# Gated delta rule plus MLP on one core: the first chunk in two halves of tokens, PSUM banks of their own, a new order

## The chip, the cores and the metric

One core of one Trainium2 chip runs the whole program. The metric is device time in microseconds (us) for one execution; lower is better. Before the change three runs took 520.83 to 522.82 us, the median 521.94.

## The reference

Two blocks follow each other. The first is a delta rule over 4 x 8 heads, 768 tokens, head size 48:

```python
k_n = k / (np.linalg.norm(k, axis=-1, keepdims=True) + 1e-06)
for t in range(S):
    kt, vt, bt = (k_n[:, :, t], v[:, :, t], beta[:, :, t, None])
    y[:, :, t] = np.einsum('bhd,bhde->bhe', q[:, :, t], state)
    v_old = np.einsum('bhde,bhd->bhe', state, kt)
    state = state + bt[:, :, :, None] * np.einsum('bhd,bhe->bhde', kt, vt - v_old)
```

Its output, with heads put side by side (384 numbers a token), is `x` of the second block:

```python
xn = (x - mu) / np.sqrt(var + 1e-06) * g_ln
ch = np.maximum(xn @ w_ch1, 0.0) @ w_ch2      # 384 -> 1536 -> 384
return x + ch
```

The weights come as 64-bit floats; everything is computed in 32 bits.

## The kernel before

The 768 tokens are cut into 12 chunks of 64. A chunk holds 64 tokens of 32 heads, two of the four batches in the upper 64 partitions and two in the lower, so a tile of MLP rows has 256 tokens (two groups g of 128 rows). Within a chunk the recurrence is written with matrices: the Gram matrix of the keys (`gram`, products L819), the inverse of a triangular matrix made from it, the product of that inverse with the values, called u, and y from u, the masked products of queries and keys (`queries`, L819 and L850) and the state.

The inverse is made in three ways. For chunk 0 `first_inverse` does it by doubling: steps n = 1 to 5, each with products E (L770), a masked copy (L775), products Z (L786), transposes on VectorE (`nat`, L735) and copies on ScalarE (`back`, L729). Step n joins blocks of 2^n tokens. For chunk 1 VectorE eliminates blocks of 16 row by row (`rows_inverse`, L907 and L914), and two joins on TensorE follow (`blocks_join` L938 to L956, `join` L970 to L999). Later chunks are eliminated in blocks of 32, two chunks at a time, with one join. The eliminated blocks go to DRAM (xd) and come back (xt<-xd) in eight transfers for chunk 1; the data to be eliminated come by gb<-gd.

`recur(c)` then does u (L1069 for chunk 0; L1052 and L1057 for chunk 1; L1088 later), y (L1095), the state (L1105), the copy of y to x, layer norm (L1139 to L1151), transposes (L1183 for early chunks) and the scaled transposed rows `xnt`. `mlp(c)` follows. For chunk 0 it has 24 tiles of 128 rows by 128 hidden units (L1406), ReLU on ScalarE (L1414), and 24 products with the second weights (L1448). Chunks 1 and 2 use 256 rows (L1426) and a product scheme with seven instead of eight block products (`seven`, L1523). From chunk 3 on the first layer uses a scheme with fifteen block products (`fifteen`, L1307).

The weights arrive in twelve pieces of 64-bit words. `fetch` loads a piece in two transfers issued by ScalarE; `convert` makes 32-bit floats of it with two ScalarE instructions (L592 hi, L600 lo), one on VectorE (L597) and one on GpSimd (L610). Pieces 0 to 5 are the first weights. Pieces 0 and 1 lie in the buffer of the hidden units, the others in three buffers of their own. Pieces 0 to 2 are converted in halves; an L1406 tile f needs the first halves for f = 0 to 2, the second halves for f = 3 to 5, pieces 3 to 5 from f = 6 on.

What sets the order: every step is recorded by `line.add` with the engine it runs on, and `ORDER`, a list of step numbers, says in which order the steps are emitted. Each engine takes its instructions in that order; waits follow from the data. Numbers count the steps as the code creates them. An "f" in the list puts in a matmul whose result nobody reads.

PSUM has eight banks: the pair `two`, the pair `by`, and f0 to f3. `PAIRS` holds them as pairs. Queries of chunk 2 and later use `two`, as do the products of keys with the state, u, the state and the Gram products; `by` holds the products of queries with the state and y.

## Time and profile before

| | |
|---|---|
| median of three runs | 521.94 us (520.83 to 522.82) |
| the profiled execution | 520.78 us, of which its span is 519.1 us |
| granted TensorE clock, mean | 0.982 |
| TensorE busy in 0 to 20, 20 to 40, 40 to 50, 50 to 60 us | 11.56, 13.59, 7.57, 7.60 us |
| DMA engines' busy share in the same stretches | 1.02, 0.74, 0.83, 0.70 |
| TensorE's last product starts its last long run | 501.88 us (82 records of L1523, 13.34 us) |
| moved | 54.56 MB, 105 GB/s over the span |

Times within the execution count from the start of the span. The profiled execution is one run; its span leaves out 1.68 us around it. A record is one instruction of the trace; most 32-bit matmuls with 128 columns of weights leave two. "issue" marks a wait for which the profile shows no cause. A busy TensorE may also be waiting between two pipelined matmuls, since their ends are modelled.

### The profile page before, as it was taken

The page shows a single profiled execution, that of the slowest core. Times are in us where ns is not written, and L with a number is a line of the kernel's source. Part 1 is how long each engine was busy: PE and PEld are TensorE (multiplying, and loading weights), DVE is VectorE, ACT ScalarE, POOL GpSimd, SP SyncE. Part 2 cuts the span into 40 slices and gives each one's busy share as a digit, 9 for nine tenths or more (in the row PEclk, how much of TensorE's full clock was granted, in tenths as well). Part 3 has the DMA queues.
Part 4 walks back from the last instruction along what each step waited for, and adds up shares of the span by engine and source line. Part 5 has one row for each costly group of instructions (what it writes and reads, how often), then busy time and mean ns, then how long its engine had stood idle before and what let it go on. Part 6 is the DMA issues. An engine that isn't in the chain of part 4 may idle for free.

```text
span 519.1 us, 22785 instructions
## 1 busy us (share of the span) xinstructions
PE 487.1 (94%) x9972; PEld 448.9 (86%) x9972; DVE 360.8 (70%) x814; ACT 206.9 (40%) x462; POOL 280.3 (54%) x447
## 2 busy tenths in 40 slices
PE   5577888999899999999999999999999999999997
PEld 4466786768798889999999989999999999999996
DVE  6577739798887567988889986757988446244241
ACT  5587845423431333234242632533513514424130
POOL 3435654604554877976764274473453742564554
PEclk9878998999999999999999999999999999999999
DMA  9957876585515866345853356643404403003011
GB/s 135 294 115 204 191 154 178 107 195 95 90 26 141 156 134 109 68 88 141 167 120 55 83 108 157 132 81 66 102 10 111 104 17 93 4 1 100 2 39 30
DMA packets 181635, 54.56 MB, mean 105 GB/s; under 512 B 164888, under 2 KB 177312, under 8 KB 181536
## 3 DMA queue, kind: packets, MB, share of 16 engines
q1 hardware_dynamic: 168512, 40.10, 37.9%
q10 hardware_dynamic: 10816, 9.83, 6.6%
q0 software_dynamic: 2208, 3.17, 3.8%
q8 instruction: 78, 1.28, 1.0%
q14 instruction: 21, 0.17, 0.1%
HBM read 36.30 MB, written 16.78 MB: 102 GB/s over the span
## 4 chain that ended last, share of the span: by engine, by line
PE 79%; DMA 5%; SPq 3%; issue 3%; DVE 3%; ACT 3%; POOL 2%; ACTq 0%; DVEq 0%; POOLq 0%
PE f L1523 27%; PE f L1307 22%; PE f L1426 6%; PE f L1448 3%; SPq L410 3%; PE two L819 3%; PE by L1033 2%; PE two L1033 2%; PE by L1095 2%; DMA xnt<-xld 2%; PE two L1088 2%; PE f L1406 1%; PE two L1105 1%; DMA words<-in_moe_w_ch_dram 1%; DMA gb<-gd 1%
## 5 line engine op out<-in xcount | busy, mean ns | idle before, releaser
L1510 POOL TENSOR_TENSOR h_all<-h_all 128x256 f32<-128x256 f32 x99 | 72.7, 745 | 30.5 <-PE f L1523 13.8
L1523 PE MATMUL f<-w_sb,h_all 128*128 128x192 f32 x396 | 82.2, 331 | 1.0 <-ACT h_all L1334 0.6
L1523 PE MATMUL f<-words,h_all 128*128 128x192 f32 x396 | 76.7, 329 | 0.0
L1523 PEld LDWEIGHTS f<-w_sb,h_all 128*128 128x128 f32 x396 | 65.1, 190 | 3.0 <-ACT h_all L1334 1.6
L1330 DVE TENSOR_TENSOR h_all<-f,h_all 128x512 f32<-128x512 f32 x72 | 48.9, 685 | 26.4 <-PE f L1307 19.3
L1523 PEld LDWEIGHTS f<-words,h_all 128*128 128x128 f32 x396 | 65.0, 190 | 1.5 <-issue 0.5
L1548 POOL TENSOR_TENSOR words<-h_all 128x128 f32<-128x128 f32 x66 | 31.2, 491 | 63.4 <-ACT h_all L1334 30.4
L907 DVE TENSOR_TENSOR tmp<-xb,gb 128x31 f32<-128x31 f32 (+19 forms) x139 | 57.5, 413 | 3.9 <-POOL xb L894 0.3
L1325 ACT COPY h_all<-f 128x512 f32<-128x512 f32 x45 | 26.2, 586 | 82.4 <-PE f L1307 68.8
L914 DVE TENSOR_TENSOR xb<-xb,tmp 128x31 f32<-128x31 f32 (+19 forms) x139 | 52.6, 378 | 3.7
L410 POOL DMA_DIRECT2D tb<-in_k_dram x64 | 42.2, 662 | 0.3 <-POOL tb L1630 0.3
L1334 ACT ACTIVATE h_all<-h_all 128x512 f32<-128x512 f32 x54 | 32.7, 626 | 23.9 <-DVE h_all L1330 23.5
L1307 PE MATMUL f<-x_new,w_sb 128*128 128x128 f32 x288 | 40.3, 278 | 0.1
L1307 PE MATMUL f<-xnt,w_sb 128*128 128x128 f32 x288 | 40.2, 277 | 0.0
L1307 PEld LDWEIGHTS f<-x_new,w_sb 128*128 128x128 f32 x288 | 36.5, 191 | 0.6 <-issue 0.2
L1307 PEld LDWEIGHTS f<-xnt,w_sb 128*128 128x128 f32 x288 | 36.5, 192 | 0.6 <-issue 0.2
L1541 DVE TENSOR_TENSOR o<-f,x 128x192 f32<-128x192 f32 x33 | 11.4, 352 | 36.8 <-PE f L1523 30.9
L1426 PE MATMUL f<-xnt,w_sb 128*128 128x256 f32 x144 | 34.5, 387 | 1.4 <-issue 1.4
L1426 PEld LDWEIGHTS f<-xnt,w_sb 128*128 128x128 f32 x144 | 26.4, 190 | 5.4 <-issue 1.8
L1523 PE MATMUL f<-w_sb,words 128*128 128x192 f32 x132 | 26.3, 329 | 0.0
L682 POOL TENSOR_TENSOR v<-v,kpair 128x768 f32<-128x768 f32 x10 | 14.7, 1473 | 14.0 <-DVE pt L897 14.0
L610 POOL TENSOR_TENSOR w_sb<-words 128x768 uint32<-128x768 uint32 (+1 forms) x11 | 14.7, 1348 | 13.7 <-ACT words L600 10.2
(239 smaller groups left out, 983.4 us busy)
## 6 DMA issues: line engine op xcount, KB each, us to landing
words<-in_moe_w_ch_dram ACTq DMA_DIRECT2D x20, 384.0 KB, 4.5
gd<-gsb SPq DMA_DIRECT2D x11, 512.0 KB, 3.9
v<-in_v_dram SPq DMA_DIRECT2D x24, 192.0 KB, 4.2
kr<-in_k_dram SPq DMA_DIRECT2D x46, 96.0 KB, 3.4
out_dram<-o SPq DMA_DIRECT2D x46, 96.0 KB, 2.2
xld<-xlt SPq DMA_DIRECT2D x9, 384.0 KB, 2.4
xnt<-xld SPq DMA_DIRECT2D x36, 96.0 KB, 2.9
tb<-in_q_dram SPq DMA_DIRECT2D x40, 64.0 KB, 2.8
```

The lines of the kernel that those rows point to most:

```text
L410: add(eng, cost, lambda: QUEUE[eng].dma_start(out=out_, in_=in_), r, w, bulk=n * ns / 16e3, np=n, **kw)
L907: lambda j=j, n=n, w=w, t=t: nc.vector.tensor_tensor(out=t, in0=xv[:, 0:n, j : j + 1].to_broadcast([128, n, w]), in1=gv[:, j : j + 1, j + ...
L914: "DVE", dve(n * w), lambda t=t, rest=rest: nc.vector.tensor_tensor(out=rest, in0=rest, in1=t, op=ALU.subtract),
L1033: nc.tensor.matmul(dst[half(e), hp, j], src[drows(hp), (e if n else key_half(c, hp, e)) * GP + j], s_all[drows(hp), e, j], start=(n == 0 o ...
L1307: nc.tensor.matmul(wide(p[:, f : f + 128]), w[:, f : f + 128], r, start=start and i == 0, stop=True, skip_group_check=True)
L1325: add("ACT", act(512), lambda: nc.scalar.copy(o, p), pk, ok)
L1330: add("DVE", dve(512), lambda: nc.vector.tensor_tensor(out=o, in0=x, in1=y, op=op), [*xk_, *yk], ok)
L1334: add("ACT", act(512), lambda: nc.scalar.activation(o, o, ACTF.Relu, scale=scale), [], ok)
L1426: nc.tensor.matmul(p[:, 0:TOK], w1_sb[:, t, f * 128 : (f + 1) * 128], xnt[:, t], start=(t == 0), stop=(t == KC - 1))
L1510: add(eng, cost, lambda: e.tensor_tensor(out=out_, in0=x, in1=y, op=op), r, w, port=2 if eng == "Pool" else 1, pr=-2)
L1523: lambda f=f, t=start and f == order[0]: nc.tensor.matmul(p[:, 0:D2], lhs(f), rhs[:, f], start=t, stop=(f == order[-1]), skip_group_check=True
L1548: lambda f=f + i: e.tensor_tensor(out=s3[f], in0=one(0, 0)[0](f), in1=one(1, 0)[0](f), op=ALU.subtract),
```

## The change

The doubling for chunk 0 stops after step 4, so it yields the inverse of two blocks of 32 tokens. The other block is handled in `first_tokens`: u of the diagonal blocks gives y, layer norm, transposes and `xnt` of the first 32 tokens of every head; the lower block's correction (products w0 and x0) is added to the same PSUM sums, and the second 32 tokens follow. The 24 tiles of chunk 0's MLP go by halves of tokens (u) instead of groups (g), with rows in two runs of 64 columns, and chunk 0's output leaves in eight transfers instead of four. The query transposes of chunk 0 move from step 2 to step 3 of the doubling, the query products from step 5 to step 4, each half of heads in a pair of banks of its own. From chunk 2 on the query products go to `by` instead of `two`, and from chunk 6 on the join's second products to the second bank of `by`. The Gram preparation of chunks 2 and 3 is created after `recur(0)`, and all of `ORDER` is new. Masks move to another buffer, and mask 5 and one set of copies (pts[1]) go.

Cut to its core:

```diff
-        for n in range(1, 6):
+        for n in range(1, 5):
...
-                if n < 5:
+                if n < 4:
                     nat(g, src, Z[2:4])
...
+    def first_queries(**kw):
+        products(0, 1, PAIRS[:2], halves=True, **kw)
+        for g in range(2):
...
+                    out=jn(pts[0])[:, :, js], in0=v[:, :, js], in1=pmask[:, None, None, :].to_broadcast([128, 2, NP, C]), op=ALU.mult,
...
     def join(c, **kw):
-        bank, ATT = (f_[2], FK[2]) if c < LATER else (by[:, 0], BY[:2])
+        banks = [(f_[2], FK[2])] * 2 if c < LATER else [(by[:, 0], BY[:2]), (by[:, 1], BY[2:])]
...
+    def first_tokens(xt, vv, vk, pt, us, x, y_j, **kw):
...
+                        nc.tensor.matmul(
+                            pu[half(e ^ hp), hp, j], xt[half(e), h], vv[half(e), h], start=(j == 0), stop=False, skip_group_check=True
+                        )
+            pe(32, prod_u, vk + [("xt", 0, g, n) for n in range(3)], pk, 0.32, name="u0", **kw)
+            add("ACT", act(384), lambda g=g, pu=pu: nc.scalar.copy(ut[:, g]..., pu), pk, [UT[g]], **kw)
+            scaled(g, pu, pk)
...
+            pe(32, prod_w, [("g", 0, g), UT[g]], [k_ for k_ in WK if k_[2] == g], 0.08, name="w0", **kw)
...
+                    "ACT" if e else "DVE", ... FK[2 + hp], [("wt", hp, e)], after=WT[hp], name="wt", **kw,
...
+        def norm_and_turn(u, banks, pk, turns):
+            rows = half(u)
...   # copies y out (ACT and DVE), statistics, sqrt, reciprocal, normalize, two transposes, xnt on DVE
+        pe(64, lambda: y_of(0, [bank_of(0), bank_of(1)]), ..., YK, 0.32, name="y0", **kw)
+        norm_and_turn(0, [bank_of(0), bank_of(1)], FK[0:2], [(f_[2], FK[2]), (f_[3], FK[3])])
+        for g, (pu, pk) in enumerate(pus):
...
+            pe(32, prod_x, ..., pk, 0.08, name="x0", **kw)
+            scaled(g, pu, pk)
+        pe(64, lambda: y_of(1, y1), ..., BY, 0.4, name="y0", **kw)
+        norm_and_turn(1, y1, [BY[:2], BY[2:]], [(two[:, 0], TWO[:2]), (two[:, 1], TWO[2:])])
...
-        for g, f in ((g, f) for g in range(0 if c else 2) for f in range(FT)):
+        for u, f in ((u, f) for u in range(0 if c else 2) for f in range(FT)):
...
-                        p[:, 0:128], w1_sb[:, t, f * 128 : (f + 1) * 128], xnt[:, t, cols], start=(t == 0), stop=(t == KC - 1)
+                        p[:, 0:128].rearrange("p (g x) -> p g x", g=2), w1_sb[:, t, f * 128 : (f + 1) * 128], tokens(xnt[:, t], u),
...
-            2: lambda: first_kt(tb[1], tb_nat(1), qts[0], ("qt", 0), PAIRS[1], pr=-99),
-            5: lambda: queries(0, PAIRS[1], halves=True, pr=-100),
+            3: lambda: first_kt(tb[1], tb_nat(1), qts[0], ("qt", 0), None, pr=-99),
+            4: lambda: first_queries(pr=-100),
...
-    prep_g(1)
     line.tag = "c0"
     recur(0, -100)
+    prep_g(1)
...
-        queries(c, pr=pr - 1, lag=0.5)
+        queries(c, PAIRS[1], pr=pr - 1, lag=0.5)
```

The new `ORDER` puts TensorE's steps of the front in this sequence: E1 (first half), chunk 1's Gram products, E1 (second half), Z1, E2, Z2, E3, the query transposes, Z3, E4, query products and Z4 by turns, u0, w0, y of the first half, x0, y of the second half, the first half's transposes, key transposes of chunk 2, the first MLP tile, chunk 2's Gram products, the second tile, the second half's transposes, key transposes of chunk 3, the third tile, chunk 3's Gram products, the state, the fourth tile. On VectorE the elimination for chunk 1 stands after the last `xnt` of the first half (before, it stood after the scaling of u), and the convert of the second half of weight piece 1 behind that elimination.

## The prediction

> **What bounds the kernel now.** I read the page first, then the table by windows, then TensorE's timeline, then VectorE's and GpSimd's up to 62 us. TensorE is busy for 94% of the span.
>
> ```profile
> PE 487.1 (94%) x9972; PEld 448.9 (86%) x9972; DVE 360.8 (70%) x814; ACT 206.9 (40%) x462; POOL 280.3 (54%) x447
> ```
>
> ```profile
> 20.00:40.00 20.00, 13.59 (x486) 11.77 (x486) 12.37 (x28) 13.61 (x31) 5.48 (x9) 0.74 0.74 185
> ...
> 50.00:60.00 10.00, 7.60 (x256) 6.61 (x250) 8.75 (x34) 8.27 (x18) 3.46 (x5) 1.00 0.70 210
> ...
> 360.00:380.00 20.00, 20.00 (x497) 19.30 (x496) 18.86 (x37) 8.67 (x18) 9.23 (x17) 1.00 0.44 93
> ```
>
> The columns are stretch, length, then busy time of PE, weight loads, DVE, ACT, POOL, granted clock, DMA share, GB/s. The loss is at the front. The late part holds none: each of the nine last chunks has 120 records of L1307 (100 take 11.3 us in the chain), 84 of L1523 (82 take 13.34 us) and eight small blocks of 0.7 to 1.1 us: 13.6 + 13.7 + 8 = 35 us; (515.2 - 202.7) / 9 = 34.7 us is what a chunk takes. So the end moves with the time at which dense work begins, which I take as chunk 1's first MLP product (L1426).
>
> ```profile
> 24.26 1.54 PE L628 MATMUL by<-ident,tb 128*128 128x128 f32 x6 [2.54 <-issue]
> 25.73 1.99 PE L786 MATMUL f<-xt,gsb 64*64 64x64 f32 x64
> ...
> 36.30 0.81 PE L786 MATMUL f<-xt 64*64 64x64 f32 x32 [0.36 <-DVE xt L775]
> 36.96 0.69 PE L770 MATMUL by<-qt,gsb 64*64 64x64 f32 x32
> ...
> 39.10 1.11 PE L819 MATMUL by<-qt,kt 48*64 48x64 f32 x64
> ...
> 46.04 0.85 PE L1069 MATMUL by<-v,xt 64*64 64x48 f32 x32
> ...
> 59.23 2.27 PE L1406 MATMUL f<-xnt,w_sb 128*128 128x128 f32 x18
> ...
> 62.93 6.21 PE L1406 MATMUL f<-xnt,w_sb 128*128 128x128 f32 x54
> ...
> 86.26 5.19 PE L1448 MATMUL f<-w_sb,h_all 128*128 128x384 f32 x10
> ...
> 114.57 10.63 PE L1426 MATMUL f<-xnt,w_sb 128*128 128x256 f32 x48
> ```
>
> Columns: start, length, what; in brackets the wait ahead of it. One sees the inverse by doubling (L770, L786), its fifth step from 36.96, chunk 0's first product u (L1069) at 46.04, its first MLP tile (L1406) at 59.23, the fourth tile at 62.93, and chunk 1's MLP at 114.57. From 62.93 to 114.57 there are 51.6 us. The work in them: 126 records of L1406 at 0.115, 14.5; 48 of L1448 at 0.325, 15.6; L944 and L949 2.7; L981 and L987 1.4; two blocks of L1033 1.9; u of chunk 1 2.2; L1095 and L1105 1.8; three of L819 3.1; L1183 0.8; sum 44.0. So 7.6 us are lost there; ten L1448 records that take 5.19 instead of 3.25 hold 1.9 of it, a wait in L987 that the profile puts down to issue 1.7.
>
> VectorE's timeline:
>
> ```profile
> 48.19 0.11 DVE L907 TENSOR_TENSOR tmp<-xb,gb 128x15 f32<-128x15 f32 x1
> ...
> 55.88 0.19 DVE L914 TENSOR_TENSOR xb<-xb,tmp 128x15 f32<-128x15 f32 x1
> ```
>
> and GpSimd's:
>
> ```profile
> 61.01 0.82 POOL L610 TENSOR_TENSOR w_sb<-h_all 128x384 uint32<-128x384 uint32 x1 [0.28 <-ACT h_all L600]
> ```
>
> VectorE's elimination for chunk 1 runs from 48.19 to 56.07. The last convert that tiles 4 to 6 need ends at 61.83.
>
> **The change, part by part.** I read the new order engine by engine, numbering the steps as the code creates them.
>
> *The fifth doubling goes.* Z4 ends at 37.11, u starts at 46.04. Ahead of u there now stand only the query products, 1.1 us on PE (L819), and three copies on ACT of 0.36. So u could start at 37.11 + 1.1 + 1.1 = 39.3.
>
> *The front.* The query transposes leave the place between E2 and Z2. Z2's operand was ready at 22.1 (L775, 21.40 + 0.73) and Z2 began at 25.73: 3.6 us, a stall of 2.54 and 1.1 of transposes. They return ahead of Z3, 1.1 to 1.5. E1's first half no longer stands behind chunk 1's products. Against that, ACT's new order puts a convert of weights ahead of the copies of Z1, and that needs two weight transfers; such a transfer took 3.5 to 7.3 us here, with the DMA engines full to 26.5 us. Bounds: 1 us lost to 6 won. I take 3.0, nearest to the 3.6 less the transposes plus E1's advance. u then starts at 36.3.
>
> *The halves of tokens.* From u to the normalized first half the new chain is VectorE's, in its order: u 1.5 on PE; two scalings 0.56 with a convert 0.94 between, 2.1 less the 0.6 under u; convert 0.42; two copies for the second block 1.0; output copy 0.5; small ones 0.4 and convert 0.7; two statistics with aggregates 1.5; scaling 0.56, reciprocal 0.17, normalize 0.48, scaling 0.56; small 0.35, convert 0.94, normalize 0.48; gb 0.41; output copy 0.5; xnt 0.37; two statistics 1.1; memset 0.27; xnt 0.37: 14.1, with some twenty hand-overs (0.07 each, an estimate) 15.5. The three new products and the second pair of transposes (about 3 us of PE, against 2.0 for the doubling's E5 and Z5) lie under that chain. Its cover is PE's idleness here; without it they would cost 1 us net. First tile: 36.3 + 15.5 = 51.8, against 59.23.
>
> *What stands behind it.* The elimination now follows xnt in VectorE's order: from 51.6. It took 7.9 with 1.8 of other work inside; the second half's normalization, 1.4, now lies inside. End 59.6. Behind it in the same queue is the convert of weight piece 1's second half (0.4 to 1.0), then GpSimd's 0.82: the fourth tile at 61.0, 1.9 sooner. But chunk 1's query transposes, its query products and its state product (1.1 + 1.16 + 1.15 = 3.4 us) were done by 62.93 and now are not. So PE is 1.5 us behind there.
>
> *From the fourth tile on.* Work 44.0 + 3.4 = 47.4. Lost: chunk 1's xnj came 13.4 us after the elimination's end; SP's new order puts the eight xt loads right behind xd and two gd, past five other transfers, 1.3 less: 71.7. PE has tiles and the moved products until 70.2, so 1.5 lost. Another 0.3 ahead of chunk 1's u, and one wait like the 1.7. The 1.9 inside L1448 goes, since its first products now stand ahead of z1 and among tiles. Sum 3.5 (bounds 2 and 7.6, today's loss). L1426 at 61.0 + 47.4 + 3.5 = 111.9, 2.7 sooner.
>
> *Priced at nothing.* Rows in two runs of 64 columns for L1406: L1307 reads runs of 32 at 0.111 a record. Four more output transfers, 0.65 each on SP at a time when it waits. Two fewer GpSimd copies (0.6) and one mask less: beside the loads. Query products in `by` and the join's second bank: PE's idle time after 115 us is about 5 us up to the tail (by the windows), which bounds what they and the new order can bring there; they could also cost 2. I take 0.
>
> *A rule against it.* After PE's stall at 21.7 the granted clock was 0.64, then 0.50 to 32 us, and 64 products of L786 took 1.99 instead of 1.40.
>
> ```profile
> 22.00:24.00 2.00, 0.00 (x0) 0.00 (x0) 0.13 (x1) 0.40 (x1) 0.00 (x0) 0.64 1.12 317
> 24.00:26.00 2.00, 1.74 (x14) 1.41 (x18) 0.00 (x0) 0.16 (x1) 0.00 (x0) 0.50 1.03 390
> ```
>
> In the new PE order nothing stands between the correction products and the second y, some 5 us. At 1.42 times, y and the transposes on the chain (2.4 us) would take 1.0 more: 520.2 instead of 519.2. The Trainium skill ("TensorE: Matmul & The Clock Gate", HAM oscillation) says that an idle gap over about 3.4 us halves the clock; the trace agrees in kind, with 2.5 us.
>
> **Sum.** The profiled execution took 520.78 (span 519.1 and 1.7 around it), 1.2 under the median of 521.94. Less 2.7: 518.1 by that execution, 519.2 by the median.
>
> **Rivals.**
>
> *Slower: the chain to the elimination is stretched.* Place: weight converts in ACT's and VectorE's queues ahead of the first half's normalization. The fetch of piece 5 is issued near 40; at 7.3 us landing instead of the median 5.1 it comes at 47.3, and its two converts (0.95, 0.9) stand ahead of the second normalize: 1.5. The same kind of wait at the front takes the 3.0 away. The clock adds 1.0. The elimination then starts at 57.1; everything behind it hangs on that one to one. It decides from 54.3 on (51.6 + 2.7). 57.1 is 2.8 slower, and with 5 lost behind instead of 3.5, 4.3: 526. For it: DMA share 1.0 to 1.2 from 4 to 26 us, PE's few fillers. Against: ACT had slack at 22 to 25 us.
>
> *Much faster: the front is undisturbed.* No stall, no wait for weights, full clock: 6 instead of 3 at the front and 2 instead of 3.5 behind: 7.2 won, 514.7. For it: the stall of 2.54 us and ten us at half clock are asked for by no arithmetic. Against: the DMA engines are full there.
>
> *It does not carry through.* Chunks 2 and 3 are eliminated on VectorE from 76 to 112 (9.14 of 10 busy at 80 to 90), their data come behind the same eight xt loads as before, and chunk 2's join waits for them: PE waits there for what it won. 521.5.
>
> **How the numbers follow.** 0.5% is 2.6 us, about what a measurement of this kernel can tell from no change. Forecast 40%, own range 516 to 522.5 (front and loss each by 2): half of it over the bound, 18% within, 2% slower. Slower rival 30%, much faster 22%, no carry 8%. So faster 42%, same 26%, slower 32%. The bounds of the much faster and the slower case, 512.5 and 528, leave out under 2 in 10.
>
> **What would show it.** Right: first L907 near 51.6, first tile near 52, fourth near 61, L1426 near 112, the late chunks at 34.7 us. Wrong: a first L907 after 54, a stall between Z1 and Z2 with ACT waiting for weights, PE idle over 5 us between 62 and 112, or late chunks that take longer.

## The result, and the profile after

The changed kernel is slower. Twenty runs of it have a median of 525.28 us (521.58 to 530.34), twenty of the kernel before beside them 521.43 (518.2 to 524.75); the ratio is 1.007, 95% interval 1.0049 to 1.0091. A second set of runs gave 1.007 (1.0037 to 1.0102). The forecast was 2.7 us faster. The profiled execution took 525.37 us, span 523.6, against 520.78 and 519.1.

The page after, TensorE's and other engines' busy time, the granted clock in 40 slices of 13 us, and the queue that brings TensorE its instructions (packets, MB, share of 16 engines):

```profile
PE 487.9 (93%) x10038; PEld 450.6 (86%) x10038; DVE 353.9 (68%) x821; ACT 206.3 (39%) x457; POOL 278.2 (53%) x445
...
PEclk9995699999999999999999999999999999999999
...
q8 instruction: 79, 1.29, 1.0%
```

And the table by windows, same columns as before:

```profile
20.00:40.00 20.00, 12.57 (x517) 10.62 (x520) 11.47 (x27) 14.69 (x38) 3.92 (x5) 0.95 0.67 156
40.00:50.00 10.00, 6.55 (x239) 5.38 (x232) 7.15 (x14) 6.12 (x12) 4.82 (x5) 0.50 0.71 151
50.00:60.00 10.00, 6.53 (x86) 5.63 (x86) 9.38 (x28) 4.33 (x8) 4.94 (x7) 0.50 0.54 146
360.00:380.00 20.00, 19.72 (x441) 19.02 (x441) 16.58 (x37) 10.04 (x22) 9.40 (x18) 1.00 0.37 86
```

In the late window TensorE is busy for 19.72 of 20 us, nearly as full as before (20.00). In 50 to 60 us TensorE is less busy (6.53 against 7.60) although its clock is half, and VectorE is full (9.38 of 10). To make the two traces comparable I split each span in three: TensorE's busy time with what was run at clock 0.50 counted half ("work"), its idle time, and the other half of the busy time at 0.50 ("half clock").

| | work | idle | half clock | span |
|---|---|---|---|---|
| before | 480.1 | 32.0 | 7.0 | 519.1 |
| after | 479.9 | 35.7 | 7.9 | 523.6 |

The split between work and half clock is only as good as the clock's rows. They begin at 20.79 us after and at 12.33 before, and the table takes the time ahead of them as full speed. It was not: 32 products of the first doubling took 1.13 us after (at 15.37, ahead of the first row) and 0.69 before (behind it), as in `f1_pool` below, whose rows begin at 12.52:

```profile
14.87 0.69 PE L770 MATMUL two<-qt,gsb 64*64 64x64 f32 x32 [0.65 <-DVE qt L758]
```

TensorE was busy for 11.32 us ahead of the first row after, for 5.97 before. Counted like the rest, this moves 5.7 us after and 3.0 before from work to half clock: the work then fell by 2.9 us and the half clock rose by 3.6. Taking half is an estimate, and for these short products it is too much: they took 1.64 times as long (1.13 for 0.69), not twice. The idle time doesn't depend on any of this.

The 3.7 us of idle time, by stretches 0 to 16, 16 to 40, 40 to 60, 60 to 90, 90 to 125, 125 to 505 us and tail: before 7.0, 7.8, 4.8, 3.7, 0.0, 4.7, 3.9; after 9.1, 7.5, 6.9, 1.4, 3.0, 3.4, 4.3. So 2.1 were lost ahead of the first doubling, 2.1 between u and the first tiles, and 0.7 net from 60 to 125 us. Of the half clock in the table, 16 to 40 us hold 3.6 before and 0.5 after, 40 to 60 us 1.6 and 6.5.

TensorE's timeline after (start, length, what; the wait ahead in brackets):

```profile
15.37 1.13 PE L774 MATMUL two<-qt,gsb 64*64 64x64 f32 x32 [0.65 <-DVE ndb L666]
...
24.27 1.15 PE L790 MATMUL f<-xt,gsb 64*64 64x64 f32 x61 [0.76 <-issue]
...
39.01 0.49 PE L790 MATMUL f<-xt 64*64 64x64 f32 x7 [3.64 <-issue]
39.24 1.10 PE L1067 MATMUL two<-v,xt 64*64 64x48 f32 x32
...
52.75 1.50 PE L1104 MATMUL by<-u,pt 64*32 64x48 f32 x64 [4.33 <-DVE u L1054]
54.19 0.90 PE L1137 MATMUL f<-ident,xln 128*128 128x128 f32 x3
...
58.88 1.49 PE L1525 MATMUL f<-xnt,w_sb 128*128 128x128 f32 x6
...
68.74 1.58 PE L1525 MATMUL f<-xnt,w_sb 128*128 128x128 f32 x12 [0.18 <-ACT h_all L1537]
...
78.01 1.53 PE L964 MATMUL f<-xnj,gsb 32*32 32x32 f32 x128 [0.18 <-DVE xnj L958]
...
93.76 1.24 PE L1573 MATMUL f<-w_sb,h_all 128*128 128x384 f32 x3 [2.53 <-issue]
...
121.46 5.45 PE L1551 MATMUL f<-xnt,w_sb 128*128 128x256 f32 x24
```

u (L1067) is 6.8 us earlier than before (46.04), but the first tile (L1525) only 0.35 (59.23), the fourth tile is 5.8 later (62.93) and chunk 1's MLP (L1551) 6.9 later (114.57). Ahead of u stands a wait of 3.64 us in the last doubling's Z products, with no releaser; ahead of the first half's transposes (L1137) stands the second half's y (L1104), which waits 4.33 for VectorE.

TensorE's own account of the 6.9 us is this. Ahead of the first tile it was idle for 23.6 us (before 19.7), from there to chunk 1's MLP for 4.5 (3.7). The other 2.3 us are busy time, and part of that is work that stood behind chunk 1's first MLP product before (394.44 us busy behind it now, 395.95 before). For what the elimination of chunk 1 leads to (L964, the first products of its join) it waited only 0.18 us.

VectorE's timeline and then GpSimd's, from the masks to the end of the elimination:

```profile
8.57 2.55 DVE L464 TENSOR_SCALAR xb<-xb 128x64 int32<-128x64 int32 x1
...
42.48 0.56 DVE L1054 TENSOR_TENSOR u<-by,bnat 128x384 f32<-128x384 f32 x1 [5.66 <-ACT x L1072]
...
46.10 1.61 DVE L904 TENSOR_SCALAR nrm_b<-nrm_b 128x16 f32<-128x16 f32 x1
...
50.86 1.38 DVE L1126 TENSOR_SCALAR xln<-x,mv,rstd 64x384 f32<-64x384 f32 x1
...
52.81 1.39 DVE L599 TENSOR_SCALAR words<-words 128x768 uint32<-128x768 uint32 x1
...
57.83 0.17 DVE L927 TENSOR_TENSOR tmp<-xb,gb 128x15 f32<-128x15 f32 x1
...
66.32 0.19 DVE L934 TENSOR_TENSOR xb<-xb,tmp 128x15 f32<-128x15 f32 x1
```

```profile
8.79 1.17 POOL L483 COPY gsb<-u 128x512 f32<-128x512 f32 x2
9.90 1.72 POOL L483 COPY xt<-u 128x512 f32<-128x512 f32 x3
...
45.33 1.47 POOL L612 TENSOR_TENSOR w_sb<-words 128x768 uint32<-128x768 uint32 x1
46.73 0.95 POOL L1788 MEMSET xt<- 128x1024 f32 x1
...
51.17 0.84 POOL L612 TENSOR_TENSOR w_sb<-h_all 128x384 uint32<-128x384 uint32 x1
...
52.84 0.95 POOL L1758 MEMSET xt<- 128x1024 f32 x1 [0.83 <-DVE db_b L908]
...
66.98 0.82 POOL L612 TENSOR_TENSOR w_sb<-h_all 128x384 uint32<-128x384 uint32 x1 [10.28 <-ACT words L594]
```

Read the two side by side: VectorE's operation on 16 columns at 46.10 lasts 1.61 us and ends as GpSimd's memset ends (47.68); the convert at 52.81, 0.56 for the same shape at 42.96, ends 0.4 behind the memset that ends at 53.79. Before, the operation on 16 columns took 0.17:

```profile
42.63 0.17 DVE L884 TENSOR_SCALAR nrm_b<-nrm_b 128x16 f32<-128x16 f32 x1 [1.06 <-ACT nrm_b L883]
```

Not every operation of VectorE is stretched so: two statistics (L1118) took 0.54 and 0.52 us at 48.90 and 49.57, the second wholly beside a GpSimd convert from 49.10 to 50.57. The elimination runs from 57.83 to 66.51, and the convert that the fourth tile needs ends at 67.80.

### The profile page after: what moved, and what is told of

Read it like the earlier page. It is cut to its first block, busy times and chain, and to the rows that moved or that the text cites. A ratio compares the mean times of both kernels' runs of the same rounds, so it can differ in the third digit from the quotient of the medians.

```text
span 523.6 us, 22932 instructions
## 1 busy us (share of the span) xinstructions
PE 487.9 (93%) x10038; PEld 450.6 (86%) x10038; DVE 353.9 (68%) x821; ACT 206.3 (39%) x457; POOL 278.2 (53%) x445
## 4 chain that ended last, share of the span: by engine, by line
PE 75%; DVE 8%; DMA 6%; ACT 5%; issue 3%; SPq 2%; ACTq 0%; DVEq 0%
PE f L1652 26%; PE f L1424 21%; PE f L1551 6%; SPq L410 2%; DMA words<-in_moe_w_ch_dram 2%; PE two L1177 2%; PE by L1177 2%; PE two L1212 2%; PE two L825 2%; PE f L1573 2%; PE by L1219 2%; PE by L825 2%; PE two L1229 1%; PE f L1525 1%; ACT es L1013 1%
## 5 line engine op out<-in xcount | busy, mean ns | idle before, releaser
L1639 POOL TENSOR_TENSOR h_all<-h_all 128x256 f32<-128x256 f32 x99 | 71.7, 742 | 19.3 <-DVE qt L934 5.8
L1652 PE MATMUL f<-w_sb,h_all 128*128 128x192 f32 x396 | 79.5, 329 | 0.0
L1677 POOL TENSOR_TENSOR words<-h_all 128x128 f32<-128x128 f32 x66 | 30.4, 482 | 55.8 <-ACT h_all L1451 22.1
L927 DVE TENSOR_TENSOR tmp<-xb,gb 128x31 f32<-128x31 f32 (+19 forms) x139 | 48.4, 348 | 3.9 <-POOL xb L914 0.4
L934 DVE TENSOR_TENSOR xb<-xb,tmp 128x31 f32<-128x31 f32 (+19 forms) x139 | 48.5, 349 | 3.6
L1551 PE MATMUL f<-xnt,w_sb 128*128 128x256 f32 x144 | 33.8, 384 | 0.3 <-issue 0.3
L1551 PEld LDWEIGHTS f<-xnt,w_sb 128*128 128x128 f32 x144 | 26.7, 190 | 4.0 <-issue 0.5
L1407 POOL TENSOR_TENSOR x_new<-xnt 128x128 f32<-128x128 f32 x27 | 12.9, 480 | 30.5 <-ACT xnt L1295 20.2
```

What stands on the lines that cost most here:

```text
L927: lambda j=j, n=n, w=w, t=t: nc.vector.tensor_tensor(out=t, in0=xv[:, 0:n, j : j + 1].to_broadcast([128, n, w]), in1=gv[:, j : j + 1, j + ...
L934: "DVE", dve(n * w), lambda t=t, rest=rest: nc.vector.tensor_tensor(out=rest, in0=rest, in1=t, op=ALU.subtract),
L1551: nc.tensor.matmul(p[:, 0:TOK], w1_sb[:, t, f * 128 : (f + 1) * 128], xnt[:, t], start=(t == 0), stop=(t == KC - 1))
L1639: add(eng, cost, lambda: e.tensor_tensor(out=out_, in0=x, in1=y, op=op), r, w, port=2 if eng == "Pool" else 1, pr=-2)
L1652: lambda f=f, t=start and f == order[0]: nc.tensor.matmul(p[:, 0:D2], lhs(f), rhs[:, f], start=t, stop=(f == order[-1]), skip_group_check=True
L1677: lambda f=f + i: e.tensor_tensor(out=s3[f], in0=one(0, 0)[0](f), in1=one(1, 0)[0](f), op=ALU.subtract),
```

## The experiments

The waits put down to "issue" have a place. Counting all of TensorE's records (products, weight loads and its few semaphore instructions), those over 0.4 us up to 100 us stand at numbers 193 modulo 256: after, 705 (1.00), 1217 (0.79), 1473 (3.85), 1985 (1.36), 3521 (0.42), 3777 (3.0); before, 705 (2.81), 1217 (0.81), 1473 (0.52), 1729 (0.72), 3777 (1.91). In brackets is the time from the start of the record before, so it is somewhat longer than the wait in the timeline. Queue q8 brings 79 packets of 16 KB for 20,206 records, one for each 256. Where TensorE waited in the first 60 us, blocks were entered 3.7 to 8.2 us apart, median 4.9 (79 cases in all runs). There the packet started 1.1 to 5.6 us (median 2.4) after TensorE had entered the block before, took about 1.05, and the first instruction ran about 1.47 after its end (1.2 to 1.7): what differs from case to case is mainly when the packet starts. The Trainium skill ("Runtime: NRT & Kernel Launch", Instruction fetch mechanics) has the blocks of 256 instructions, each engine's own queue for them, and a crossing that is "mostly hidden". The trace agrees on block and queue; here the crossing is not hidden, since 256 records of 64-column products are run in less than 4.9 us.

Theories: (S) the supply of instructions sets when u can start, so operands that are ready earlier bring nothing; (V) VectorE's chain behind u, stretched beside GpSimd and lengthened by what is queued in it, sets the first tile; (A) the slower rival of the prediction: weight converts in ACT's and VectorE's queues; (C) the clock. The recorded expectations use letters of their own and say what each stands for. Step numbers below are those of `ORDER`. Ratios are to the kernel before, with 95% intervals; the changed kernel's own is 1.007.

### Supply of instructions, and the front

```diff
  e1_shift, ORDER: 32 times f (on 64 x 64) ahead of 97, the first key transposes of chunk 1
+            nc.tensor.matmul(banks_of[key[:2]][0:64, 0:64], ident[0:64, 0:64], ident[0:64, 0:1].to_broadcast([64, 64]))
```

> The changed kernel with 32 products of 64x64 more on TensorE, ahead of the transposes of chunk 1's keys, where TensorE idles 1.6 us; they go to a bank that is written anew. Question: what is the wait of 3.64 us that the profile puts down to issue, in the middle of Z4? Theory A, blocks: TensorE's instructions come in blocks of 256 (the instruction queue has one 16 KB packet for each), and a block that lands late holds TensorE up wherever its first instruction happens to stand. In the changed kernel all waits of over 0.4 us that are put down to issue stand at the same place modulo 256 of TensorE's records (705, 1217, 1473, 1985, 3777: each 193 over a multiple). Then the waits move 64 records forward in the order: the one in Z4 stands ahead of its last 39 products instead of its last 7. Rival: the wait belongs to the product it stands at (bank, operand, semaphore): it stays ahead of the last 7. Time: within 1.5 us of the changed kernel (525.3) under both.

Ratio 1.0229 (1.0174 to 1.0284). Each f left two products and two weight loads, so the blocks moved by 128 records, not by 64; and the 64 products cost 0.11 each, 7.0 us, not the time I had expected, so the run says little on the size. On the question it does: the wait ahead of Z4's last seven products is gone, so it doesn't belong to them, and the waits further on stand at 193 modulo 256 again (3265 to 17857), with other products there. At 3777 it was L1573, now it is L1001:

```profile
92.00 0.67 PE L1001 MATMUL f<-xnj,gsb 32*32 32x32 f32 x55 [0.89 <-issue]
```

E1 came 4.6 later (19.98) and u only 2.25 later (41.49), and every wait at a block's border before 60 us was gone (0.0 to 0.1): from E1 to u it took 21.5 instead of 23.9 us. With the front held back, the instructions were there in time. From 125 to 505 us 9.1 us were idle instead of 3.4; that I can't explain.

```diff
  e2_quiet, ORDER (ACT: two weight transfers out of the time of Z4, their converts with them)
- 168 90-91 160 ... 297 216 ... 241 217 242 218
+ 289 90-91 ... 298 216 ... 303 217 ... 304 218
```

> The changed kernel with the two weight transfers that ACT issues at 31.55 and 31.96 us (piece 3) moved in ACT's queue behind the copies of u, to some 41 us, and the converts of that piece a few places later. Theory A, blocks: the block of instructions that Z4 waits for is fetched while these transfers hold the DMA engines (busy from 33.0 to 35.6), so the wait of 3.64 us falls below 1.5, u starts 2 to 3 us sooner than 39.2, the granted clock does not halve at 38 us, chunk 1's MLP (L1551) starts near 118.5 instead of 121.5, time near 522.5. Theory B, VectorE's queue: from the scaling of u at 42.5 to 66.7 us VectorE is full, and the elimination for chunk 1 stands behind it; u sooner by 2 to 3 us still moves the elimination by as much, so time near 522.5 too, unless the converts that now come later put back what was won (then 525). If the wait does not fall, A's account of why the block is late is wrong.

Ratio 1.0068 (1.0038 to 1.0099). The wait at record 1473 was 2.01, u 37.73, L1551 120.99. The second profile of the unedited kernel had by chance 2.75, u 38.15 and L1551 119.20, so this is within chance: why a block takes as long as it does is not told by it.

```diff
  f1_pool, ORDER (GpSimd's five copies L483 behind VectorE's masks)
- 661 37-39 42 40 2
+ 112 37-39 42 40
```

> The changed kernel with GpSimd's five copies of the unit block (L483, 8.79 to 11.62 us) moved behind VectorE's second masking of kt (L756), where the kernel before has them. Theory P, the port: in the changed kernel a VectorE operation on 64 columns of integers (L464), 0.2 us elsewhere, takes 2.55 us from 8.57 to 11.12, while these copies run, and chunk 0's scaled keys stand behind it. Without the copies it takes 0.2 us, the first doubling (L774) starts at 13.0 to 13.5 instead of 15.37, and TensorE idles 7 us instead of 9.1 in the first 16. If the front carries to the end, the time is 523 (2 sooner than the changed kernel). Rival, blocks: the doublings then run into the fetch of TensorE's instructions sooner; u comes less than 1 us sooner than 39.2, and the time stays at 525.

VectorE's and TensorE's timelines of this run:

```profile
7.90 0.28 DVE L464 TENSOR_SCALAR xb<-xb 128x64 int32<-128x64 int32 x1
```

```profile
12.57 0.69 PE L774 MATMUL two<-qt,gsb 64*64 64x64 f32 x32
...
23.95 1.98 PE L790 MATMUL f<-xt,gsb 64*64 64x64 f32 x61 [2.27 <-issue]
...
39.58 0.34 PE L790 MATMUL f<-xt 64*64 64x64 f32 x7 [2.50 <-issue]
39.82 1.10 PE L1067 MATMUL two<-v,xt 64*64 64x48 f32 x32
```

The mask operation that took 2.55 us takes 0.28, and E1 starts 2.8 earlier. Nothing of it reaches u, 39.82 against 39.24: waits at borders before 60 us sum to 9.0 instead of 6.6. Ratio 1.0102 (1.0039 to 1.0165). What was won ahead of the first block came back as waits for instructions, as (S) has it.

`f4_both` makes both edits.

> The changed kernel with GpSimd's five copies later, as in the run with these alone, and the two weight transfers moved behind the copies of u, as in the run with those alone (there the wait in Z4 fell from 3.6 to 2.0 us and u came 1.5 us sooner, but the half clock went on to 65.8 us and the time stayed). If front, fetch and end hang together one to one, u starts near 35.5, the elimination near 55, L1551 near 118.5, time 521.5 to 522.5. If the half clock and the weights take it back, u is 3 us sooner and the time still 524.5 or more.

Ratio 1.0106 (1.0046 to 1.0166): E1 13.13, u 38.93, elimination 58.33, L1551 120.72. No gain of the one stands beside the other.

```diff
  g1_wide (after) and g2_bwide (before): chunk 1's 64 Gram products are left out, eight wide ones stand in their place
+                    nc.tensor.matmul(o, ident, kt[:, g * NP : (g + 1) * NP].rearrange("p j t -> p (j t)"))
+                    nc.tensor.matmul(o.rearrange("p (j t) -> p j t", t=C), ident, ident[:, None, 0:C].to_broadcast([128, NP, C]))
```

> The changed kernel with the 64 small products of chunk 1's keys with themselves (L825, 1.93 us at 16.28) replaced by 8 products of 256 columns into the same two banks (about as long on TensorE, 0.22 us each); this part of the computation is left out, the rest runs on what they write. Question: what paces the front? Theory S, supply: up to 48 us TensorE is paced by the arrival of its instructions, 256 to a block, each block entered 4.3 to 6 us after the one before it: the block with record 1473 was entered at 38.9 us in the kernel before, 39.0 in the changed one, 39.6 where the first doubling came 2.8 us sooner. With 112 instructions fewer ahead of u, u comes 112/256 of a block sooner, about 2.0 us: near 37.0 instead of 39.2; chunk 1's MLP near 119.5, time near 523.3. Rival, the doublings' own chain (VectorE's transposes and masks, ACT's copies): TensorE's time is the same, so u stays at 38.7 to 39.5 and the time at 525.

> The kernel before with the same replacement (64 small products of chunk 1's keys, L819 at 12.46, by 8 wide ones; this part of the computation left out). Theory S, supply: u 1.5 to 2 us sooner than 46.04, time 520 to 520.5 by its own comparison. Rival, the doublings' chain: u within 0.5 us, time as before.

`g1_wide`: 1.0125 (1.0084 to 1.0166); `g2_bwide`: 1.0035 (0.9999 to 1.007). The eight wide products cost some 3 us more than the 64 small ones, so no time was won and the totals tell nothing. The stretch behind them does: from Z1 to u it took 18.2 us (21.65 to 39.86) against a mean of 21.0 (19.3 to 22.1) in nine runs with the changed kernel's order of TensorE up to u, and in the kernel before 25.6 to u's products in `two`, against 29.6 and, in `f3_join`, 32.2. With fewer records in the blocks, the same products came faster, and the waits before 60 us fell to 2.0.

```diff
  g3_glate (created behind u; numbers as in the changed kernel)
- gram(1): 100-103 between E1's halves, 104 and 231-238 (gd) with it, y 297 behind w0
+ 288 100 101 297 ... 289 102 103 ... gd loads, preparation 239-243 later
```

> The changed kernel with the 64 products of chunk 1's keys behind u instead of between the doublings, the first y ahead of the products w, and the loads of gb and VectorE's preparation of the elimination correspondingly later. Nothing is left out. Theory S, supply: half a block fewer instructions ahead of u: u near 37, the first tile near 56.7 instead of 58.9; the elimination near 56 to 58 (its last load of gb is expected at 52 to 55). L1551 near 119.5, time 523. If the loads of gb come after 56, the elimination starts at 59 to 60 instead of 57.8 and the time is 525 to 526. Rival, the doublings' chain: u at 39, everything behind it later by the moved products, 526.

TensorE's timeline of it, then VectorE's:

```profile
30.79 0.34 PE L790 MATMUL f<-xt 64*64 64x64 f32 x7 [0.74 <-issue]
...
37.59 1.01 PE L1067 MATMUL two<-v,xt 64*64 64x48 f32 x32 [1.23 <-ACT xt L733]
...
59.25 1.06 PE L1525 MATMUL f<-xnt,w_sb 128*128 128x128 f32 x4
```

```profile
46.35 2.21 DVE L599 TENSOR_SCALAR words<-words 128x768 uint32<-128x768 uint32 x1 [0.30 <-ACT words L594]
48.49 0.54 DVE L1118 BATCH_NORM_STATS2 st<-x 64x6 f32<-64x384 f32 x1
```

Now u waits for a copy on ACT, not for instructions. Over three runs with this edit (here, `i2_gconv`, `j2_gturns`) u stands at 37.59, 36.50, 35.37, mean 36.5; over the nine with chunk 1's products ahead, at a mean of 39.6 (38.15 to 40.88). Taking 128 records out of the way, half a block, brings u 3.1 earlier: the size that the prediction had given to operands. It isn't the products' own time, since they stand ahead of Z1, and from Z1 to u it is 18.1 instead of 21.0. Part of that can be the clock: its rows put 0.0 to 0.5 us of half clock into 16 to 40 us in these three runs, 0.5 to 4.2 in the nine. But the first tile is at 59.25, and the ratio 1.0113 (1.0063 to 1.0163).

### From u to the first tile

```diff
  e4_elim, ORDER (VectorE): preparation and elimination 239-275 between u and the normalizations; 206 and 207 earlier, 207 ahead of 318; the loads of xt (277-284) right behind the store of xd
  e5_convert, ORDER
- 357 206 340 ... 353 207 328
+ 206 317 ... 207 246 (the elimination's first)
```

> The changed kernel with the elimination for chunk 1 (L927, L934) begun ahead of u's scaling, in the 5.7 us in which VectorE idles, and the rest of its pairs spread between the steps of the first half's layer norm, instead of all behind the first half's last xnt; its eight loads of xt right behind the store of xd. Theory B, VectorE's queue: chunk 1's inverse is what the dense part waits for. The elimination ends near 59.5 instead of 66.5, the join (L1001) starts near 82.5 instead of 88.7, L1551 near 117, time 520 to 522; the first tile of the MLP may come up to 3 us later (61 instead of 58.9). Theory A, the wait and the half clock on TensorE alone: both stay as they are, and the end moves by less than 1 us: 524.5 to 526.

> The changed kernel with one convert of VectorE, 0.42 us (second half of weight piece 1), moved from behind the elimination to ahead of it, with its counterpart on ACT. The fourth tile of chunk 0's MLP waits for it through GpSimd. Expected: that tile starts at 62 to 65 instead of 68.74. If TensorE's supply at 60 to 70 us is what counts, the end comes 2 to 3 us sooner (522.5). Theory B, chunk 1's path from the elimination: TensorE only waits later instead, and the time stays within 0.8 us of the changed kernel.

`e4_elim`: 1.0144 (1.0109 to 1.0179). The elimination ran from 44.29 to 62.87, but u's second scalings slid to 55.38, the first tile to 62.77 and L1551 to 126.14. VectorE has one queue there, and it is full: what goes first delays the other. `e5_convert`: 1.0089 (1.0055 to 1.0123), and no test of what it was made for, since GpSimd's half of the convert still stood behind the elimination in time:

```profile
68.44 0.83 POOL L612 TENSOR_TENSOR w_sb<-h_all 128x384 uint32<-128x384 uint32 x1 [10.26 <-DVE xb L934]
```

```diff
  i1_conv, ORDER: 217 behind 315 and 225 behind 309 (VectorE's two converts behind the scalings and the first xnt)
  i2_gconv: i1_conv and g3_glate together
  i3_prep: i1_conv, and the preparation 32 239-243 245 and the first two row pairs 246-249 ahead of chunk 0's statistics
```

> The changed kernel with two of VectorE's converts (L599, pieces 3 and 5, 0.97 and 1.39 us) moved in its queue: one from ahead of the first half's statistics to behind the scaling of its correction, one from ahead of the second normalize to behind the first half's last xnt. Theory B, VectorE's queue: these are the converts that the prediction's slower rival named; with them out of the way the statistics (L1118) start at 47.2 instead of 48.9, the first tile comes 1.5 to 2.3 us sooner than 58.9, the elimination 0.8 to 1.5 sooner than 57.8, L1551 near 120, time 0.3 to 0.4% under the changed kernel. Theory S, supply of instructions: the second half's correction products (record 1985) and the second y are late anyway; but the first half does not need them, so the first tile moves as B says only if nothing of the first half's chain waits for TensorE.

> The run with the products of chunk 1's keys behind u, and the same two converts moved. There u came at 37.35 instead of 39.2 and the first half's output copies at 43.9 instead of 45.6, but the statistics stood until 48.5 behind a convert that took 2.2 us beside GpSimd's, and the first tile came at 59.0 as before. If that convert was what took the 1.9 us back, the statistics start near 45, the first tile near 55.5 to 56.5, L1551 near 118.5, time 521.5 to 522.5 (1.0 of the kernel before). If the gain stops elsewhere (the loads of gb at 53.7, the second y), the first tile still comes at 58 or later and the time is 1.007 or more of the kernel before.

> The changed kernel with the two converts moved, and the preparation of the elimination (L904 to L908, L917, 2.6 us of VectorE in the first profile) and its first two pairs ahead of the first half's statistics, where VectorE idles 5.7 us before u is scaled. Theory B, VectorE's queue: the first tile 2 to 3 us sooner than 58.9 (56 to 57), the elimination's end 3 to 4 sooner than 66.5, L1551 near 118.5, time 521.5 to 522.5. If TensorE's instructions and the second weights (its wait at 90 us) set what follows, the first tile comes sooner and L1551 does not: 1.006 of the kernel before or more.

Ratios 1.0101 (1.0061 to 1.0141), 1.0132 (1.0084 to 1.018) and 1.0109 (1.0074 to 1.0143). The first tile is at 59.25, 60.44 and 59.03. In `i1_conv` no convert stands between the output copies and the statistics (0.97 us in the changed kernel) or between the two normalizations (1.39); three (0.55, 0.42, 0.54) still stand ahead of the first one. Much of what was freed so went into operations that stayed, beside GpSimd: the normalizations took 1.70 and 1.19 (1.38 and 0.65 in the changed kernel), L908 0.87 (0.15). Nor does a wait for a weight transfer stand ahead of VectorE's converts at 47.92 and 52.81 in the changed kernel. So (A) isn't borne out as what decides. `i3_prep`'s TensorE timeline, and two lines of VectorE's, show what is late next:

```profile
53.21 1.51 PE L1104 MATMUL by<-u,pt 64*32 64x48 f32 x64 [3.03 <-DVE u L1054]
54.64 0.90 PE L1137 MATMUL f<-ident,xln 128*128 128x128 f32 x3
...
59.03 1.49 PE L1525 MATMUL f<-xnt,w_sb 128*128 128x128 f32 x6
```

```profile
50.98 1.70 DVE L1126 TENSOR_SCALAR xln<-x,mv,rstd 64x384 f32<-64x384 f32 x1
...
53.08 1.05 DVE L1126 TENSOR_SCALAR xln<-x,mv,rstd 64x384 f32<-64x384 f32 x1
```

The transposes (L1137) follow the second half's y (L1104) at once. The first three were ready at 52.68, where the first normalization ends, and stood behind y in TensorE's queue; the other three had to wait for the second normalization, to 54.13. In the changed kernel the two ends are 52.24 and 54.77, and y runs from 52.75: there too y holds up only the first three.

```diff
  j1_turns, ORDER: step 316 (second half's y) behind 569 (first tile); on VectorE both normalizations ahead of the second scaling of u, the preparation behind it
  j2_gturns: the same on g3_glate
```

> The changed kernel with the first half taken apart from the second in the queues: on TensorE the first half's transposes (L1137), the transposes of chunk 2's keys and the first tile stand ahead of the second y (L1104), on VectorE the first half's statistics and both normalizes ahead of the second scaling of u, one convert and the elimination's preparation behind them. In the changed kernel TensorE's queue has the second y, which waits for the correction products (held up at record 1985) and VectorE's second scaling until 52.75, ahead of the first half's transposes (54.2); moving converts alone did not move the first tile (19.4 us behind u, as before). Theory O, the order: the first half hangs on the second half's chain. Then the statistics start at 46.5, the first transposes at 49 to 50, the first tile at 51.5 to 54, 13 to 15 us behind u as the prediction had it, the elimination near 54 to 55, L1551 near 118.5, time 0.4 to 0.8% under the changed kernel. Rival: VectorE is full from 42 us on, so what comes sooner there pushes the second half, the elimination and the weights back by as much; the first tile comes sooner, L1551 and the time stay.

> The same on top of the run with the products of chunk 1's keys behind u, in which u comes 1.9 us sooner. Theory O: the first tile at 50 to 53 us, the elimination at 55 to 57 (the loads of gb come near 54), L1551 near 118, time at or under the kernel before. Rival: first tile sooner, the time still 0.7% or more over the kernel before.

TensorE's timeline of `j1_turns`, and VectorE's of `j2_gturns`:

```profile
50.58 0.90 PE L1137 MATMUL f<-ident,xln 128*128 128x128 f32 x3 [0.84 <-DVE xln L1126]
...
56.39 1.49 PE L1525 MATMUL f<-xnt,w_sb 128*128 128x128 f32 x6
57.81 1.51 PE L1104 MATMUL by<-u,pt 64*32 64x48 f32 x64
...
63.72 1.98 PE L825 MATMUL f<-kt 48*64 48x64 f32 x64 [4.41 <-ACT kt L637]
65.63 1.65 PE L1525 MATMUL f<-xnt,w_sb 128*128 128x128 f32 x6
```

```profile
51.06 1.73 DVE L904 TENSOR_SCALAR nrm_b<-nrm_b 128x16 f32<-128x16 f32 x1 [0.63 <-ACT nrm_b L903]
...
53.61 1.39 DVE L908 TENSOR_TENSOR db_b<-db_b,beta_f 128x16 f32<-128x16 f32 x1
```

`j1_turns` has the first tile 16.4 us after u (56.39 after 40.01), near the 15.5 of the prediction. The edit changes TensorE's order and VectorE's together (both normalizations are done by 50.91, in the changed kernel by 54.77), so about 3 of the 19.6 us lie in the two orders; what each is worth was not separated. It doesn't pay: the second tile is at 65.63 (62.02 in the changed kernel), since TensorE then waits 4.41 for key copies, the elimination ends at 69.74, L1551 is at 124.99, and the ratio 1.0134 (1.0089 to 1.018). `j2_gturns`, u at 35.37, loses the time on VectorE: two operations on 16 columns take 3.1 us together, the first tile comes at 57.19, the elimination runs from 58.06 to 70.53, and the ratio is 1.0167 (1.0127 to 1.0206).

### The clock

```diff
  f2_warm, ORDER: f 3 times ahead of 292, 10 ahead of 316, 3 ahead of 338 and of 337
  h_warm2, ORDER: f 8 times ahead of 316, into a bank that nobody reads then
+            bank = f_[3]
```

> The changed kernel with 19 pairs of products of 128x128 (0.22 us a pair at full clock) that compute nothing needed, on TensorE where it idles between 42 and 58 us: 3 pairs ahead of w (L1086), 10 ahead of the second y (L1104), 6 ahead of the transposes of chunk 2's keys. Theory C, the clock: in the changed kernel the granted clock is 0.50 from 38 to 61.7 us; counted as full-speed work, idle time and what the half clock adds, the span is 480 + 35.7 + 7.9, and 6.5 of the 7.9 lie between 40 and 60. Kept busy, TensorE is back at 1.00 by 48 us; the half clock adds under 2.5 us there; L1551 starts 2 to 3 us sooner than 121.5, time 522.5. Theory B, VectorE's queue: the clock comes back but the chain from u to the first tile is VectorE's and ACT's, so what the half clock no longer adds comes back as idle time: 525 to 526.

> The changed kernel with 8 pairs of products of 128x128 that compute nothing needed behind the correction products, ahead of the second y, this time into a bank that is free there (in the run with 19 pairs the ten in this place waited for VectorE to read the bank that y writes, and stood in y's way for 4.6 us). Theory C, the clock: TensorE is busy from 44 to 51 us, the granted clock is back at 1.00 by 52 to 55 us instead of 61.7, the half clock adds 2 us less, time 523.5. Theory B, VectorE's queue: the first tile comes less than 0.7 us sooner than 58.9, since what it waits for there is VectorE's; time 524.5 to 525.5.

`f2_warm`: 1.0286 (1.0229 to 1.0343), TensorE's timeline:

```profile
50.61 4.64 PE L1728 MATMUL by<-ident 128*128 128x128 f32 x20 [1.38 <-DVE u L1054]
```

The fillers waited themselves for VectorE's reading of their bank, and then stood ahead of y at half clock. `h_warm2` mends that: idle in 40 to 60 us falls from 6.9 to 4.1, but clock 0.50 lasted from 40.1 to 53.8, half clock still took 5.8, and the ratio is 1.0141 (1.0105 to 1.0177). The fillers (48.10 to 51.88) no longer held y up, which waited for VectorE until 52.35. The first tile came at 58.07, 0.8 sooner, yet L1551 at 124.28, 2.8 later; why is not shown. What the half clock alone costs was not separated.

### Banks, and a repeat

```diff
  f3_join, on the kernel before, its order unchanged
-        bank, ATT = (f_[2], FK[2]) if c < LATER else (by[:, 0], BY[:2])
+        banks = [(f_[2], FK[2])] * 2 if c < LATER else [(by[:, 0], BY[:2]), (by[:, 1], BY[2:])]
```

> The kernel before with one part of the change alone: the second products of the join of chunks 4 and later write a PSUM bank of their own. The prediction priced it at nothing, with bounds of 2 us to both sides. Expected: within 0.3% of the kernel before. If the copies of the first products had held up the second, TensorE's idle time between 125 and 505 us (4.7 us before) falls by up to 2 us.

Ratio 1.0031 (0.9991 to 1.0071): no gain. Idle from 125 to 505 us is 4.1 against 4.7. The query products in `by` hang on the new order and were not tried alone. This run's profile is of use for another reason. By chance it waited 11.5 us at borders of blocks before 60 us (before: 4.7); u came at 49.18 (46.04 in the first profile), the first tile at 64.06 and L1426 at 117.39, 2.8 later than in the first profile, and its span is 520.9, only 1.8 longer.

`i0_again` is the changed kernel, unedited.

> The changed kernel once more, beside the three below. Expected: 1.005 to 1.009 of the kernel before; in the profile u near 39 us, the first tile of the MLP near 59, the elimination from 57.8, the half clock somewhere between 38 and 66 us. What differs from the first profile shows how much of a single profile's difference is chance: the waits for blocks of instructions (3.85 us at record 1473, 1.36 at 1985, 3.0 at 3777) are expected at the same records, with other lengths.

Ratio 1.007 (1.0037 to 1.0102). Its profiled execution is one of the quick ones (522.51, span 520.8): u 38.15, elimination 56.73 to 65.43, L1551 119.20, half clock 5.4. So single profiles of this kernel differ by 2 to 3 us through the front; differences of that size between two profiles prove nothing. The readings of `e1_shift`, `f1_pool` and `g1_wide` above are of one profile each; for them speak the sums of the waits (0.0, 9.0 and 2.0 us, 6.6 and 5.8 in the two profiles of the unedited kernel) and, for `e1_shift` and `g1_wide`, a stretch from Z1 to u (18.4 and 18.2) shorter than in any of the nine runs. Of TensorE's idle time, two differences hold in second profiles too, `i0_again` after and `f3_join` with the order of before: 9.1 against 7.2 in 0 to 16 us, 7.1 against 4.9 in 40 to 60.

No version was faster than the kernel before.

## Why the prediction was wrong

**The fifth doubling: right as a step, lucky as a number.** u was to start at 39.3 without the term for the front, right behind Z4; it started right behind Z4, at 39.24. But the 3.64 us of waiting ahead of Z4's last seven products are in no term of that sum, and over the nine runs u came between 38.15 and 40.88.

**The front, 3.0 us: failed.** u was to come to 36.3 and did not. The term took a stall for a matter of operands ("Z2's operand was ready at 22.1"), removed it, and asked what was late next only in ACT's queue. It was a wait at record 705, at a border of a block, and its like came back at 1473 as long as TensorE ran ahead of its instructions. That the records, not the operands, set u is shown by `f1_pool` (E1 2.8 earlier, u not) and `g3_glate`, `i2_gconv`, `j2_gturns` (half a block fewer, u 3.1 earlier in the mean). The hint stood in the prediction's own lines: "[2.54 <-issue]" names no operand. The sign to be seen if weights were the cause, ACT waiting for them between Z1 and Z2, was not there.

**The chain from u to the last xnt of the first half, 15.5 us to the first tile: mis-sized.** It took 19.6. By the legs of the sum: u and the scalings were put at 3.0 and took 4.7 (39.24 to 43.97; the products ran at half clock, and the first scaling stands behind ACT's copy of the same sums); from there to the statistics 3.0 and 4.9 (L904's 1.61 beside GpSimd and a convert of 0.97); statistics 1.5 and 1.3; to the end of the normalizations 3.5 and 4.5 (1.38 and 1.39 beside GpSimd); then 3.0 and 3.15; hand-overs, 1.5, are in the measured legs; at the end 1.0 more for chunk 2's key transposes, ahead of the tile in TensorE's queue. The sum of durations was from rows in which GpSimd happened to be quiet (before, it was idle from 47.9 to 56.5 us). That the waits beside GpSimd are what stretched the legs is read from the traces, not tried by taking GpSimd's work away there; `f1_pool` tried it at another place.

**"The three new products ... lie under that chain": failed in part.** Their work did lie under it, but the second half's y went ahead of the first half's transposes with a wait of 4.33 for VectorE, and held up the first three of them. With it put behind, and VectorE's order changed with it (`j1_turns`), the first tile is 16.4 after u.

**The elimination "from 51.6", end 59.6; fourth tile 61.0.** Measured 57.83, 66.51 and 68.74. The start is 6.2 late, 3.0 from the front and 3.2 from the chain; the elimination took 8.7 instead of 8.0 (the terms that the prediction names, 7.9 less 1.8 and 1.4 more, make 7.5), and what stands behind it 2.2 instead of 1.4. That it follows the first half's xnt held. That the fourth tile hangs on it was not seen: the convert ended at 67.80, but TensorE was at work until 68.56 on products that stand behind the first tile now, and waited 0.18 us more, for ScalarE. Before, the elimination began 2.2 us after u (48.19 after 46.04); now 18.6 us after u, so the 6.8 us that u gained are less than the 16.4 it was moved back. Yet its lateness alone cost TensorE no more than the 0.18 us ahead of L964. Moved forward again (`e4_elim`) it delays the first half instead.

**From the fourth tile on, 47.4 of work and 3.5 lost, 50.9:** 52.7 measured (51.6 in `i0_again`), with 3.4 of idle time. L1551 was to be at 111.9 and is at 121.46: of these 9.6 us 7.1 were lost ahead of the first tile (51.8 predicted, 58.88 measured).

**"So the end moves with the time at which dense work begins": failed in size.** L1551 moved by 6.9, the end by 4.5. The late chunks took 34.61 each (predicted 34.7), so they are not it; behind L1551 there is 1.5 less work (busy 394.44 against 395.95), which now stands ahead of it, and 0.9 less idle time. `f3_join` shows the same on the kernel before.

**Banks at 0:** borne out for the join (`f3_join`, between 0.1% faster and 0.7% slower), not tried for the queries.

**The rivals.** "Slower" gave 526 with an elimination at 57.1, and this is nearly what came: 57.83 and 525.28. That is chance: its mechanism is not what the runs showed. No wait for weights was seen there, and with two of VectorE's converts moved back (`i1_conv`, `i3_prep`) the first tile stayed at 59. Its rule of the clock came in part: 0.50 from 37.85 to 61.75, though the prediction looked for it at the second y. It fell 2.5 us into the wait of 3.64 (which began at 35.37); before, 0.9 us into the wait of 2.54 (21.72, clock 0.50 from 22.57). That agrees in kind with the Trainium skill ("TensorE: Matmul & The Clock Gate", HAM oscillation), but both times the clock fell sooner than after the 3.4 us of idling that the prediction quotes. What it cost here was not separated. "Much faster" needed a front without a wait, and "no carry" would have had the tile early and chunk 2 late; neither was seen.

**Open.** Why one block takes 3.7 and another 8.2 us, that is, why its packet starts sooner or later, was not found. And the ratio of `g3_glate`, whose u came at 37.59, is 1.0113 (1.0063 to 1.0163), no better than the changed kernel's 1.007: an earlier u alone did not shorten the time. The traces put that loss between u and the first tile, where VectorE is full, but no edit there gave the time back, so what causes it is argued, not shown. The half clock, which the new front has more of, remains a rival for part of it.

## What to carry to other kernels

A wait that names no releaser is not won back by bringing operands earlier: count the records of its engine and see whether such waits recur at a fixed distance; if they do, fewer instructions in that stretch can help (here they moved u, though not the time). When a step is cut into halves, count instructions and not elements on the engine that has them in series, and see whether a half that waits stands in another engine's queue ahead of one that could go. Where operations of one engine take longer while another works, as VectorE's did beside GpSimd, take durations for a sum from rows in which the neighbour is as busy as it will be.

## What the runs showed of the hardware

**TensorE's instructions come in blocks of 256 records, and it runs ahead of them.** Waits to 4.25 us (`f3_join`, record 705) stood at record numbers 193 modulo 256, in each kernel; where TensorE waited, the packet for the next block had started 1.1 to 5.6 us (median 2.4) after the block before was entered.

**Some operations of VectorE wait out GpSimd, over several of its instructions.** An operation of 0.28 us (`f1_pool`) took 2.55 while GpSimd ran its copies, and operations on 16 columns, 0.15 to 0.25 us elsewhere, took 1.39 to 1.73. The Trainium skill ("SBUF — State Buffer", SBUF: two separate sides) says of the port pair that the two engines share that it is an exclusive lock: a VectorE operation of certain kinds (in a mode that takes two ports, or with two inputs from SBUF) or GpSimd's holds it for the whole instruction, and "the other fully blocks". The trace agrees in kind: statistics (0.52) and copies from PSUM (0.55) took their usual time beside GpSimd. And here the wait went through more than one instruction of GpSimd: the 1.61 us at 46.10 began beside a convert and ended with the memset behind it.

**Half of the partitions cost VectorE the same time.** Statistics on 64 partitions x 384 took 0.52 to 0.54 us, on 128 before 0.55; so halves of tokens double the time of these steps.

**Small fillers aren't cheap.** In `e1_shift` 64 products of 64 x 64 with one column broadcast took 7.03 us, 0.11 each, where the kernel's own 32 products of 64 x 64 a little later took 1.13, 0.035 each.
